# When x and the last halves of U's sums are loaded for the first pair of a Winograd-multiplied token MLP, and the buffer in which one end is made

## The chip, the cores and the metric

One core of one Trainium2 chip. The metric is the device time of one execution in microseconds (us); before the change the median of three runs is 703.48 us (702.54 to 704.59). Everything is float32; matrix products go through TensorE as fp32r, with each operand split into a high part and the rest, so that one product is three matmuls (high by high, high by rest, rest by high).

## The reference, cut to what matters

```
sa, ca, ga, sb, cb, gb = modulation rows made from c
h = layernorm(x) * (1 + ca) + sa            # x: 2048 tokens x 640 channels
x = x + ga * A(h, k, v, ...)                # short conv, gate, long conv by FFT
h = layernorm(x) * (1 + cb) + sb
u = gelu(h^T @ w1 + b1)                     # 640 x 1728, over the tokens
y = (u @ w2 + b2)^T                         # 2048 x 640
out = x + gb * y
```

The change lies in the last two lines: U times w2, and the ends `out = x + gb * (y + b2)`. By then x (after the first residual) is in DRAM, in `xs`.

## The kernel before, in words

Instructions stand in program order on each engine; nothing is rescheduled. Up to 503 us the kernel computes the convolution, the norms and U, one block of 128 of the 1728 hidden units after the other (`FS`, matmuls at L437). The last block ends at 515.8 us. From there on the matmuls at L1074 multiply U by w2, in eight **pairs** of 128-token blocks. A pair is a 2 x 2 block product, done with seven products instead of eight (Winograd's form). So a pair needs sums of w2's four quarters A11, A12, A21, A22 (`sums`, on VectorE), which are then split (`prep`: high part on ScalarE at L1011, rest on VectorE at L1012, shown as L60), and it needs sums of U's quarters (`TU`), made once.

**The products.** `product(n)` does the 56 products, seven for each pair: for n = 0 to 6 in the order A11, A12, S4, S1, S2, S3, A22 (`FIRST`). Each sums over seven sets of hidden units (`SETS`, three matmuls each, 21 in all) into one PSUM buffer. Products take the four PSUM buffers of a ring in turn: product n+4 writes where product n wrote, so it waits until product n has been read. The weights of product n+3 reuse the slot of those of product n.

**U's sums.** For the five sets 6, 0, 1, 2, 3 the sums were made early and saved to DRAM (`ts`), because there was no room. They come back (`t_back` L897, and L1051, L1064 for set 6) in ten transfers of 640 KB: first the halves `T13` (used by S1 and S3), then the halves `T42` (used by S2 and A22). The last two of the ten are set 3's second half, into `h_x` (L1063, shown as L897), and set 6's second half, into `m_x` (L1064). Product 4 (S2) is the first that reads the second halves. Sets 4 and 5 are made in place (`t_sums`, `t_split`), set 5 late, while the first products run.

**The ends.** `outcome(n)` follows product n. For the first pair: A11 is copied to `p1` by ScalarE (L1093); S1 to `p5` (L1095); A12 is finished by VectorE (`finish`: L1083, times gb, plus x at L1085) in the buffer `o1` and stored (L1086); S2's outcome makes `u2 = S2 + p1`, then `o1 = u2 + p5`, and finishes with it the bank of product 2 (S4), again in `o1`, plus x[1]; and so on. `p1, p5, u2, u3, o1` and the first of the x buffers are 320-column pieces of one tile, `m_w1`, so all of them appear in the trace as `m_w`.

**x.** `x_pair(p)` loads the four x pieces (160 KB each) of pair p; two sets of four buffers take turns. The second pair's last three buffers lie in `m_p`, over the working space of U's sums.

**SP's queue.** All transfers here are issued by SyncE (SP) in program order. In the built program every transfer has one of eight completion semaphores in turn, and SP issues a transfer only when the eighth before it has landed. SP also waits at a store until VectorE has made what is stored, with all later loads behind it. The order before, from the last sums on: ..., set 2's second half (`r_z`), `x_pair(0)` (4), set 3's second half, set 6's second half, A11 and A12 of pair 1 (4 transfers), `x_pair(1)` (4), the store of A12's end, A21 and A22 of pair 1 (4), the further stores.

Of the kernel before, what the change touches and what calls it, by code (L numbers as in the profile page):

```python
# [12 lines left out]
ALU = mybir.AluOpType  # L13
# [37 lines left out]
def mixer_kernel(ctx: ExitStack, tc: tile.TileContext, q, k, v, shift_k, ssm_k, ssm_D, w1, b1, w2, b2, c,  # L51
# [7 lines left out]
    act, dve, pool, pe, sync = nc.scalar, nc.vector, nc.gpsimd, nc.tensor, nc.sync  # L59
    TT = lambda eng, o, a, b, op: eng.tensor_tensor(o, a, b, op=op)  # L60
# [10 lines left out]
    def psum(slot=None):  # L71

        uid[0] += 1
        slot = ring[uid[0] % len(ring)] if slot is None else slot
        return psp.tile([128, 1024], F32, name=f"pst_{uid[0]}", tag=f"pst{slot}", bufs=1)
# [315 lines left out]
    def load_w2(t, s, f0):  # L391

        sync.dma_start(t[:, 0:6, :], dram(w2, fo(f0) * S + 128 * s, [[S, 128], [128 * S, 6], [1, 128]]))
        sync.dma_start(t[:, 6, :], dram(w2, fo(f0 + 6) * S + 128 * s, [[S, 128], [1, 128]]))
# [479 lines left out]
    def t_sums(i):  # L874

        hi, lo = full[7 + i]
        TT(dve, TW[:, 640:1280], hi, lo, ALU.add)
        TT(dve, T13, span2(TW, 320, 640), span2(TW, 0, 320), ALU.subtract)
        TT(dve, TW[:, 960:1280], TW[:, 960:1280], T13[:, 0], ALU.subtract)
        TT(dve, TW[:, 640:960], TW[:, 640:960], TW[:, 960:1280], ALU.subtract)  # L880
# [13 lines left out]
    def t_back(i, k):  # L894

        t, n = H[JS[i][k]][0], SAVED.index(i)
        sync.dma_start(bass.AP(tensor=t.tensor, offset=t.offset, ap=[t.ap[0], [1, 1280]]),  # L897
                       ts[128 * n:128 * n + 128, 1280 * k:1280 * k + 1280])

    def t_split(i):  # L900

        for k, t in enumerate((T13, T42)):
            act.activation(span2(H[JS[i][k]][0], 0, 640).bitcast(F32R), t, AF.Copy)
        for k, t in enumerate((T13, T42)):
            TT(dve, span2(H[JS[i][k]][0], 320, 640).bitcast(F32R), t, span2(H[JS[i][k]][0], 0, 640), ALU.subtract)
# [58 lines left out]
    def load_pair(p, n0=0, n1=4):  # L964

        if p < NP:
            for n in range(n0, n1):
                w_ = ("A11", "A12", "A21", "A22")[n]
                A[p, w_] = place[(4 * p + n) % 8]
                load_w2(A[p, w_], 2 * p + int(w_[1] == "2"), 7 * int(w_[2] == "2"))  # L970

    W, bank, slots, place = {}, {}, [], [q7(X, 0), q7(X, 896)]
    Q = lambda n, i: U[7 * (n // 2) + i]
    moving = {"A11": lambda i: Q(0, i)[0::2], "A12": lambda i: Q(2, i)[0::2], "S4": lambda i: Q(2, i)[1::2],
              "S1": lambda i: TU[i][0], "S2": lambda i: TU[i][1], "S3": lambda i: TU[i][2], "A22": lambda i: TU[i][3]}
    SETS = (4, 0, 1, 2, 3, 6, 5)
    FIRST = ("A11", "A12", "S4", "S1", "S2", "S3", "A22")
    ORDER = ("A11", "A12", "S1", "S2", "S3", "S4", "A22")
    of = lambda n: (n // 7, (ORDER if n > 6 else FIRST)[n % 7])
# [1 line left out]
    def x_load(s, h, t):  # L981
        sync.dma_start(t, xs[128 * s:128 * s + 128, 320 * h:320 * h + 320])

    def x_pair(p):
        if p < NP:
            for n in range(4):
                x_load(2 * p + n // 2, n % 2, xq[4 * (p % 2) + n])

    def sums(n):

        p, w_ = of(n)
        if p >= NP:
            return
        a = lambda k: A[p, k]
        if w_ == "S1":
            A[p, w_] = S1 if p else place[6]
            TT(dve, A[p, w_], a("A21"), a("A22"), ALU.add)
        elif w_ == "S2":
            TT(dve, a("A21"), a("A11"), a("A21"), ALU.subtract)
            TT(dve, a("A11"), a("S1"), a("A11"), ALU.subtract)  # L1000
            A[p, "S3"], A[p, "S2"] = a("A21"), a("A11")
        elif w_ == "S4":
            TT(dve, a("A12"), a("A12"), a("S2"), ALU.subtract)
            A[p, "S4"] = a("A12")

    def prep(n):

        p, w_ = of(n)
        if p < NP:
            W[n] = slots[n % 3]  # L1010
            act.activation(W[n][0].bitcast(F32R), A[p, w_], AF.Copy)  # L1011
            TT(dve, W[n][1].bitcast(F32R), A[p, w_], W[n][0], ALU.subtract)  # L1012

    for f_ in FS:
# [18 lines left out]
        if f_ == FS[-1]:  # L1033
# [13 lines left out]
            t_, n = thirds(m_x, 8, 1792), SAVED.index(6)  # L1047
# [11 lines left out]
    m_w1 = mem(f"w{WB[12]}", 4096, "m_w1")  # L1059
    p1, p5, u2, u3, o1, *xq = thirds(m_w1, 10, 896) + thirds(m_p, 3)  # L1060
    S1 = q7(m_w1, 0)
    x_pair(0)
    t_back(3, 1)  # L1063
    sync.dma_start(m_x[:, 3072:4352], ts[128 * n:128 * n + 128, 1280:2560])  # L1064
    load_pair(1, 0, 2)

    def product(n):
        w_ = of(n)[1]
        bank[n] = psum()[:, 0:320]
        wh, wl = W.pop(n)  # L1070
        for m, i in enumerate(SETS):
            rh, rl = moving[w_](i)
            for k, (w, r) in enumerate(((wh, rh), (wh, rl), (wl, rh))):
                pe.matmul(bank[n], w[:, i].bitcast(F32R), r.bitcast(F32R), start=m == 0 and k == 0,  # L1074
                          stop=m == 6 and k == 2)

    def finish(s, h, t, o, x, u=None):

        g = GB[:, 320 * h:320 * h + 320]
        if u is None:  # L1080
            dve.scalar_tensor_tensor(o, t, B2C[:, s:s + 1], g, op0=ALU.add, op1=ALU.mult)
        else:
            dve.scalar_tensor_tensor(o, t, B2C[:, s:s + 1], u, op0=ALU.add, op1=ALU.add)  # L1083
            TT(dve, o, o, g, ALU.mult)
        TT(dve, o, o, x, ALU.add)  # L1085
        sync.dma_start(out[128 * s:128 * s + 128, 320 * h:320 * h + 320], o)  # L1086

    def outcome(n):

        p, w_ = of(n)  # L1090
        t, s, x = bank[n], 2 * p, xq[4 * (p % 2):4 * (p % 2) + 4]
        if w_ == "A11":
            act.activation(p1, t, AF.Copy)  # L1093
        elif w_ == "S1":
            act.activation(p5, t, AF.Copy)  # L1095
        elif w_ == "A12":
            finish(s, 0, t, o1, x[0], p1)
        elif w_ == "S2":
            TT(dve, u2, t, p1, ALU.add)
            if p == 0:  # L1100
                TT(dve, o1, u2, p5, ALU.add)
                finish(s, 1, bank[2], o1, x[1], o1)
        elif w_ == "S3":
            TT(dve, u3, t, u2, ALU.add)
            if p:
                TT(dve, u2, u2, p5, ALU.add)
            finish(s + 1, 1, u3, p5, x[3], p5)
            if p == NP - 1:
                TT(dve, u3, u3, GB[:, 0:320], ALU.mult)
                TT(dve, u3, u3, x[2], ALU.add)  # L1110
        elif w_ == "S4":
            if p:
                finish(s, 1, t, u2, x[1], u2)
        elif p == NP - 1:
            finish(s + 1, 0, t, o1, u3)
        else:
            finish(s + 1, 0, t, u3, x[2], u3)

    for n in range(7 * NP):
        if n == 1:  # L1120
            t_sums(5)
        if n:
            prep(n + 2)
        if n == 1:
            t_split(5)
            x_pair(1)
        if n == 2:
            outcome(1)
        if n > 3:
            sums(n + 3)  # L1130
        product(n)
        if n != 1:
            outcome(n)
        if n == 2:
            load_pair(1, 2, 4)
        if n % 7 == 6:
            load_pair(n // 7 + 2)
            x_pair(n // 7 + 2)
# [6 lines left out]
def build(inputs):  # L1145
    import concourse.bacc as bacc

    nc = bacc.Bacc("TRN2", target_bir_lowering=False, num_devices=1)
    arrays, args = {}, []

    def add(name, a):
        a = np.ascontiguousarray(a)
        arrays[f"in_{name}_dram"] = a
        args.append(nc.dram_tensor(f"in_{name}_dram", a.shape, mybir.dt.from_np(a.dtype), kind="ExternalInput").ap())

    for name in _INS:
        a = np.asarray(inputs[name])
        add(name, a.reshape(S, D) if name in ('A_q', 'A_k', 'A_v') else a)
    for name, a in _constants().items():
        add("const_" + name, a)  # L1160
    args.append(nc.dram_tensor("out_0_dram", (S, D), F32, kind="ExternalOutput").ap())
    with tile.TileContext(nc) as tc:
        mixer_kernel(tc, *args)
    return nc, arrays
# [8 lines left out]
```

## Time and profile before

| | |
|---|---|
| median of three runs | 703.48 us (702.54 to 704.59) |
| the profiled execution's own time | 698.38 us |
| its span in the profile | 696.6 us |
| TensorE (PE) busy | 636.1 us, 91% |
| VectorE (DVE) busy | 510.4 us, 73% |
| ScalarE (ACT) busy | 312.7 us, 45% |
| mean granted TensorE clock | 0.98 (1.00 in every stretch from 440 us on) |

Lines of a timeline read: start (us), duration, engine, line, operation, out<-in, shapes, count; in brackets the engine's idle time before it and what released it. PE is the matmuls, PEld the weight loads beside them, SPq an issue on SP's queue; the duration of several issues in one line includes the waits between them. The chain of waits gives start, length and the work or the transfer that the end hung on. Matmul ends are modelled: starts are what to go by.

### The profile page before, as it was taken

Reading aid. Unit: us, or ns where it says so; the run is one execution under the profiler, and the core shown is the slowest. Engines: PE = TensorE matmul, PEld = TensorE weight load, DVE = VectorE, ACT = ScalarE, POOL = GpSimd, SP = SyncE. Lnnn points to the kernel's source line nnn. Section 1 sums busy time; section 2 is a strip of 40 time slices with the busy share of each in tenths; the row PEclk is TensorE's granted clock in tenths of the full one; section 3 lists DMA queues with packets and bytes.
Section 4 is the critical chain, followed back from the end, with each engine's and each line's share of the span. In section 5 each row is a group of like instructions: output and inputs, shape, how many; then the busy total and the mean of one; then the engine's idle time right before and its main releaser. Section 6 shows DMA issues by size and latency. Waiting matters only on the chain.

```text
span 696.6 us, 20710 instructions
## 1 busy us (share of the span) xinstructions
PE 636.1 (91%) x9057; PEld 615.6 (88%) x9057; DVE 510.4 (73%) x857; ACT 312.7 (45%) x467; POOL 154.9 (22%) x137
## 2 busy tenths in 40 slices
PE   0699978889999999987899999999998999999997
PEld 0699668889999989776899999999997999999997
DVE  7778559969879637888895420675586898988886
ACT  0664574635645545645766421532433333333331
POOL 5288039625526427200000000000000000000000
PEclk9999899999999899999999999999999999999999
DMA  9978888546333513352113651578499644455511
GB/s 183 218 221 256 303 159 169 129 78 145 69 65 87 174 45 82 116 135 49 30 32 59 124 97 25 128 182 216 148 320 302 182 127 128 130 171 173 162 49 39
DMA packets 173553, 95.91 MB, mean 138 GB/s; under 512 B 89716, under 2 KB 163223, under 8 KB 173463
## 3 DMA queue, kind: packets, MB, share of 16 engines
q1 hardware_dynamic: 168914, 93.28, 51.6%
q10 hardware_dynamic: 4548, 1.31, 1.1%
q8 instruction: 71, 1.16, 0.7%
q14 instruction: 20, 0.16, 0.1%
HBM read 77.53 MB, written 17.04 MB: 136 GB/s over the span
## 4 chain that ended last, share of the span: by engine, by line
PE 62%; DVE 15%; POOL 8%; DMA 7%; ACT 4%; issue 2%; SPq 2%; ACTq 0%; DVEq 0%; POOLq 0%
PE pst L1074 22%; PE pst L437 17%; PE pst L230 7%; POOL y L60 6%; PE pst L246 5%; PE pst L275 5%; PE pst L939 3%; DVE tap L60 3%; DMA aux<-in_A_ssm_k_dram 2%; DVE kt L60 2%; DMA h_a<-ts 1%; SPq L164 1%; DMA m_x<-ts 1%; POOL t L60 1%; DMA in<-in_A_k_dram 1%
## 5 line engine op out<-in xcount | busy, mean ns | idle before, releaser
L246 PEld LDWEIGHTS pst<-z,w 128*64 128x64 f32 x2560 | 94.7, 141 | 9.2 <-ACT z L232 7.3
L246 PE MATMUL pst<-z,w 128*64 128x64 f32 x2560 | 96.0, 240 | 7.5 <-ACT z L232 6.1
L60 POOL TENSOR_TENSOR y<-p 128x256 f32<-128x256 f32 x72 | 91.6, 1328 | 23.6 <-DVE p L60 23.2
L60 DVE TENSOR_TENSOR p<-pst,kt 128x512 f32<-128x512 f32 x80 | 52.5, 691 | 21.9 <-ACT kt L250 13.5
L230 PE MATMUL pst<-v,x 128*64 128x128 f32 x640 | 46.6, 307 | 23.5 <-DVE x L60 23.5
L230 PEld LDWEIGHTS pst<-v,x 128*64 128x64 f32 x640 | 44.6, 221 | 24.1 <-POOL t L462 23.5
L232 ACT ACTIVATE z<-pst 128x1024 f32<-128x1024 f32 x40 | 45.9, 1148 | 40.1 <-PE pst L230 22.2
L275 PEld LDWEIGHTS pst<-v,y 32*128 32x128 f32 x1280 | 40.4, 197 | 6.8 <-POOL y L60 3.6
L250 ACT ACTIVATE kt<-pst 128x512 f32<-128x512 f32 x40 | 25.2, 630 | 47.0 <-PE pst L246 24.9
L275 PE MATMUL pst<-v,y 32*128 32x64 f32 x1280 | 42.4, 283 | 3.6 <-DVE y L60 2.8
L1074 PE MATMUL pst<-r_z,m_w 128*128 128x320 f32 x198 | 37.5, 310 | 2.5 <-DVE m_w L1083 2.5
L230 PE MATMUL pst<-v,p 128*64 128x128 f32 x640 | 37.4, 274 | 2.3 <-ACT p L176 1.6
L230 PEld LDWEIGHTS pst<-v,p 128*64 128x64 f32 x640 | 35.1, 137 | 3.3 <-ACT p L176 1.7
L60 DVE TENSOR_TENSOR tap<-tap,kt 128x512 f32<-128x512 f32 x51 | 35.6, 698 | 1.3
L60 DVE TENSOR_TENSOR kt<-in,tap 128x512 f32<-128x512 f32 x51 | 35.0, 687 | 1.5
L1074 PEld LDWEIGHTS pst<-r_z,m_w 128*128 128x128 f32 x198 | 31.1, 188 | 2.9 <-issue 2.7
L283 ACT ACTIVATE z<-pst 128x512 f32<-128x512 f32 x38 | 21.3, 661 | 25.6 <-PE pst L275 25.6
L1011 ACT ACTIVATE m_w<-m_v 128x896 fp32r<-128x896 f32 x19 | 17.9, 949 | 25.9 <-DVE m_v L60 14.9
L1074 PE MATMUL pst<-h_x,m_w 128*128 128x320 f32 x132 | 26.5, 309 | 0.0
L294 PEld LDWEIGHTS pst<-z,v 64*64 64x64 f32 x1280 | 21.1, 139 | 5.8 <-issue 3.1
L437 PE MATMUL pst<-r_z,wb 128*128 128x320 f32 x144 | 23.1, 317 | 2.6 <-DVE aux L60 1.7
L60 DVE TENSOR_TENSOR m_w<-m_v,m_w 128x896 fp32r<-128x896 f32 x19 | 20.7, 1088 | 6.5 <-ACT m_w L1011 6.5
(300 smaller groups left out, 1426.0 us busy)
## 6 DMA issues: line engine op xcount, KB each, us to landing
x<-in_B_w_dram SPq DMA_DIRECT2D x20, 512.0 KB
m_v<-in_B_w_dram SPq DMA_DIRECT2D x20, 384.0 KB
aux<-in_A_ssm_k_dram SPq DMA_DIRECT2D x10, 512.0 KB
out_dram<-m_w SPq DMA_DIRECT2D x32, 160.0 KB
in<-in_A_k_dram SPq DMA_DIRECT2D x36, 128.0 KB
in<-in_A_v_dram SPq DMA_DIRECT2D x36, 128.0 KB
ts<-m_p SPq DMA_DIRECT2D x10, 320.0 KB
m_w<-xs SPq DMA_DIRECT2D x20, 160.0 KB
```

Source lines behind the costliest of these rows:

```text
L60: TT = lambda eng, o, a, b, op: eng.tensor_tensor(o, a, b, op=op)
L230: pe.matmul(ps[64 * ri:64 * ri + 64, o:o + 128], lhs, F1[:, 128 * ri:128 * ri + 128], start=True, stop=True)
L232: evac = lambda: act.activation(Z[:, side, t].rearrange("p a k e -> p e a k"), ps.rearrange("p (e a k) -> p e a k", a=8, e=2), AF.Copy)
L246: pe.matmul(ps[64 * h:64 * h + 64, o:o + 64], W2[k1 // 32][:, 2 * (k1 % 32) + ri], rhs, start=True, stop=True)
L250: act.activation(kt.rearrange("p (m i) -> p m i", i=32), pv[:, :, 1], AF.Copy)
L275: pe.matmul(pp[qd // 2][:, o:o + 64], Y[p, ri, i:i + 2].rearrange("p i k -> p (i k)"), V2[p, 64 * ri:64 * ri + 64], start=ri == 0, stop=ri ...
L283: act.activation(o, i, AF.Copy)
L294: pe.matmul(ps[64 * b:64 * b + 64, 512 * e + 64 * jj:512 * e + 64 * jj + 64], V1[p, ri, n2], T2[p, :, 32 * ri + n2], start=ri == 0, stop=r ...
L437: pe.matmul(ps[0:m, h, 0:320], w_.bitcast(F32R), r_[:, 320 * h:320 * h + 320].bitcast(F32R), start=first and i == 0, stop=last and i == 2)
L939: pe.matmul(ps[n][:, h, 0:320], sets[n][:, j].bitcast(F32R), r[:, 320 * h:320 * h + 320].bitcast(F32R), start=j == 0 and r is hh, stop=j = ...
L1011: act.activation(W[n][0].bitcast(F32R), A[p, w_], AF.Copy)
L1074: pe.matmul(bank[n], w[:, i].bitcast(F32R), r.bitcast(F32R), start=m == 0 and k == 0, stop=m == 6 and k == 2)
```

## The change

For the first pair, `x_pair(0)` is issued after the second halves of sets 3 and 6 instead of before them. `x_pair(1)` is issued after all four quarters of pair 1 (and so after the first store), instead of between A12 and the store. From product 4 on, set 6 (which lies in `m_x` for S1, S2, S3 and A22) is multiplied last and set 5 before it; products 0 to 3 keep the order. In the first pair S2's end is made in `p1` instead of `o1`.

```diff
-    SETS = (4, 0, 1, 2, 3, 6, 5)
+    SETS = (4, 0, 1, 2, 3)
...
     S1 = q7(m_w1, 0)
-    x_pair(0)
     t_back(3, 1)
     sync.dma_start(m_x[:, 3072:4352], ts[128 * n:128 * n + 128, 1280:2560])
+    x_pair(0)
     load_pair(1, 0, 2)
...
-        for m, i in enumerate(SETS):
+        for m, i in enumerate(SETS + ((6, 5) if n < 4 else (5, 6))):
...
             if p == 0:
-                TT(dve, o1, u2, p5, ALU.add)
-                finish(s, 1, bank[2], o1, x[1], o1)
+                TT(dve, p1, u2, p5, ALU.add)
+                finish(s, 1, bank[2], p1, x[1], p1)
...
         if n == 1:
             t_split(5)
-            x_pair(1)
...
         if n == 2:
             load_pair(1, 2, 4)
+            x_pair(1)
```

In the order of the built programs this moves the eight x loads on SP's queue and the last two sets of the products from the fifth on; the instructions on VectorE, ScalarE and GpSimd stand in the same order and number as before. The `p1` that the first pair's S2 end now occupies is written again by ScalarE's copy of A11 of the second pair (L1093), which therefore waits for that end's store.

## The prediction, on record before the changed kernel ran

> **What bounds the kernel now.** I read the windows first, for the stretch in which TensorE stops; then the chain of waits over the last 240 us, for what ends each stop; then the timelines of PE, VectorE and SP around it. Windows (us, then busy time and count of PE, PEld, DVE, ACT, POOL, then granted clock, DMA share, GB/s):
>
> ```profile
> 520.00:540.00 20.00, 16.63 (x112) 16.11 (x111) 13.98 (x21) 7.55 (x11) 0.00 (x0) 1.00 0.93 316
> ```
>
> PE stands for 3.37 us (20.00 - 16.63) while the first pair's products run, at full clock. The chain says why:
>
> ```profile
> 523.20 8.19 DMA m_x<-ts
> ...
> 532.80 3.62 DMA out_dram<-m_w
> ...
> 536.87 0.50 DVE m_w L60
> ...
> 537.40 0.56 DVE m_w L1083
> ...
> 538.10 154.49 PE pst L1074 x1050
> ```
>
> From 538.10 on the chain is PE's matmuls (154.49 us) and the last end behind them: what is won ahead of 538.10 is won at the end, as long as nothing else becomes late. PE's timeline, starts being what counts:
>
> ```profile
> 525.04 1.04 PE L1074 MATMUL pst<-r_z,m_w 128*128 128x320 f32 x6
> ...
> 528.12 0.60 PE L1074 MATMUL pst<-r_z,m_w 128*128 128x320 f32 x3
> ...
> 529.89 0.62 PE L1074 MATMUL pst<-h_x,m_w 128*128 128x320 f32 x3
> 531.43 0.70 PE L1074 MATMUL pst<-m_x,m_w 128*128 128x320 f32 x3 [0.92 <-DMA m_x<-ts]
> ...
> 538.10 0.68 PE L1074 MATMUL pst<-r_z,m_w 128*128 128x320 f32 x3 [2.45 <-DVE m_w L1083]
> ...
> 550.49 0.84 PE L1074 MATMUL pst<-r_z,m_w 128*128 128x320 f32 x3
> ```
>
> A product without a stop takes 528.12 - 525.04 = 3.08 us, a set of three matmuls 0.44. Product 4 starts at 528.12. Two stops follow: **stop A**, in product 4, until set 6's second half lands (531.43 where 529.89 + 0.44 = 530.33 was due: 1.10 us); **stop B**, ahead of product 6, until VectorE has read the bank of product 2 (L1083). Without stops product 6 would start at 528.12 + 2 x 3.08 = 534.28; it starts at 538.10, 3.82 later. A third, tiny one is in product 10 at 550.49: its first three matmuls take 0.84 for the usual 0.60, 0.24 us.
>
> **Part 1: S2's end in p1.** VectorE's timeline:
>
> ```profile
> 528.16 0.49 DVE L60 TENSOR_TENSOR m_w<-m_w 128x320 f32<-128x320 f32 x1
> 528.57 1.08 DVE L60 TENSOR_TENSOR m_x<-m_v,m_x 128x896 fp32r<-128x896 f32 x1
> 529.64 1.09 DVE L60 TENSOR_TENSOR m_w<-m_v,m_w 128x896 fp32r<-128x896 f32 x1
> ...
> 536.87 0.49 DVE L60 TENSOR_TENSOR m_w<-m_w 128x320 f32<-128x320 f32 x1 [3.77 <-DMA out_dram<-m_w]
> ...
> 538.92 1.08 DVE L60 TENSOR_TENSOR m_w<-m_v,m_w 128x896 fp32r<-128x896 f32 x1
> 539.92 0.48 DVE L60 TENSOR_TENSOR m_w<-pst,m_w 128x320 f32<-128x320 f32 x1
> 540.44 0.55 DVE L1083 SCALAR_TENSOR_TENSOR m_w<-m_w,sm 128x320 f32<-128x320 f32 x1
> ...
> 542.96 1.08 DVE L60 TENSOR_TENSOR m_w<-m_v,m_p 128x896 f32<-128x896 f32 x1
> ...
> 549.77 1.09 DVE L60 TENSOR_TENSOR m_w<-m_v,m_w 128x896 fp32r<-128x896 f32 x1 [1.08 <-ACT m_w L1011]
> ```
>
> 528.16 adds x[0] to A12's end in o1; its store is issued at 532.80 and out at 536.42 (3.62 in the chain); only then may 536.87 write o1 again, and L1083, which frees the bank, comes after it at 537.40. In p1 there is no store to wait for: p1's last reader is u2, one instruction earlier on the same engine. So stop B's cause goes. What is late next is VectorE's own queue.
>
> **Part 2: x behind the last halves.** SP's timeline:
>
> ```profile
> 516.62 3.75 SPq L982 DMA_DIRECT2D m_w<-xs  x4
> 521.64 0.32 SPq L897 DMA_DIRECT2D h_x<-ts  x1
> 523.20 0.32 SPq L1064 DMA_DIRECT2D m_x<-ts  x1
> 524.79 0.38 SPq L393 DMA_DIRECT2D m_v<-in_B_w_dram  x1
> 526.38 0.33 SPq L394 DMA_DIRECT2D m_v<-in_B_w_dram  x1
> 526.83 0.38 SPq L393 DMA_DIRECT2D m_v<-in_B_w_dram  x1
> ```
>
> Each issue waits for the eighth transfer before it, so issues tell landings: 521.64, 523.20, 524.79 and 526.38 are the landings of set 6's first half and of three further 640 KB halves, 1.58 us apart. The transfers move one behind the other at 655 KB / 1.58 us = 415 GB/s; the path is full, and issuing earlier gains nothing, only standing earlier in line does. 526.83 is the eighth after x[0], so x[0] landed at most 0.45 us after the half ahead of it. Now the line is: last r_z half 526.35, h_x 527.9, m_x 529.5 (before 531.4), x[0] 529.95, x[3] near 531.4, which is m_x's landing before (the same bytes in all).
>
> Stop A: m_x is now there at 529.5, and set 5 first puts its use at 529.89 + 0.88 = 530.77. It goes, with 1.3 us to spare. The reordered sets themselves cost nothing: the same 21 matmuls; h_x, needed at 529.89, lands at 527.9.
>
> The price: x[0]. Call T the start of its addition, 528.16 before, when x[0] had been there for 1.3 us. Now T is its landing: from 529.95 (above) to 531.4 (it cannot be later than x[3], whose place in the bytes is m_x's of before). I take T = 530.1, near the lower end, since 0.45 is the row nearest to it; 0.15 for the semaphore and for m_x's slowness at 531.38 where 1.58 steps give 531.1. So this is an added wait of some 1.9 us on VectorE. Queued behind it: the rest of prep(5) (528.57), that of prep(6), then S2's outcome. From the rows: prep(5)'s rest at T + 0.41 = 530.5, ending 531.6; prep(6)'s at T + 1.48; u2 at T + 2.48 (1.00 as from 538.92 to 539.92); the addition in p1 0.52 later (539.92 to 540.44), T + 3.00 = 533.1; L1083 at 533.6, ending 534.2. From the addition on everything stands 536.87 - 533.1 = 3.77 us earlier than before.
>
> PE: product 5 starts at 531.20; its third matmul (531.50) needs prep(5)'s rest at about 531.75: 0.25 lost. Product 6 could start at 534.53; the bank is free at 534.2 plus 0.14 (537.96 to 538.10): no wait. That is 3.57 gained, and 0.08 more from the first matmuls after stop B (0.68 for 0.60). Products 7 to 9 follow without a stop.
>
> Product 10 needs prep(10)'s rest: 549.77 before, the last of a VectorE queue that has no pause from 536.87 but the 1.08 us it waits for ScalarE behind its own sum. This queue moves by 3.77, PE by 3.65; before, PE lost 0.24 there, now 0.12. So the gain behind product 10 is that of the queue, **3.77 us**. It cannot exceed 3.82 + 0.24 = 4.06 (no stop at all), and with T = 531.4 it is 536.87 - 534.4 = 2.5.
>
> [...]
>
> **Part 3: x of the second pair behind its weights.** A21 and A22 are issued right behind the first store, x_pair(1) after them; as each waits for the eighth before, the last part of A22 waits for A11's first, which had landed by 533.07:
>
> ```profile
> 533.07 0.95 ACT L1011 ACTIVATE m_w<-m_v 128x896 fp32r<-128x896 f32 x1 [3.46 <-DMA m_v<-in_B_w_dram]
> ```
>
> So A22's last issue is near 533.1. VectorE first needs these quarters for S1's sum, 542.96 before, 539.2 now (less 3.77): 6 us behind the issue. x_pair(1), issued next, is first needed behind product 8, whose end PE reaches at 534.5 + 3 x 3.08 = 543.8. What hides both is that VectorE and PE have the first pair to work on; nothing gained, nothing lost. Were that cover gone, VectorE's queue would lose one for one.
>
> Part 3 also delays p1's store, behind x_pair(1) and T: made by 533.6 + 1.52 = 535.2 (537.40 to 538.92), landed near 538.8 by the 3.62 of the chain. ScalarE writes p1 again with product 7's outcome, which ends at 534.5 + 2 x 3.08 = 540.7. Covered by 1.9 us.
>
> **Sum.** 698.38 - 3.77 = 694.6 us for an execution like the profiled one (span 692.8); the median of the runs stood 5.1 above the profiled time, the same kernel: 703.48 - 3.7 = **699.8 us**. About 0.3%, 2.1 us, is what a measurement of this kernel can tell from no change.
>
> **Rivals.**
> *x[0] late* (0.10): the stop on PE is exchanged for one on VectorE. For it: each 160 KB load could pay a landing of its own instead of the 0.45; the isolated store took 3.62 from issue to landing, T = 529.5 + 3.62 = 533.1 and a gain of 0.8 us (702.7). Against: x[0] is issued between 516.62 and 521.64, at least 8 us ahead, while the line is full. Above T = 531.8 the gain is under 2.1. [...]
> *A21 and A22 late* (0.03), the side of slower: they stand behind a store that now waits for T. VectorE holds at S1's sum, 539.2, one for one; from a landing at 543.0 on the change is slower than before, by over 0.3% from 545.1 (705.6). Against: issued by 533.1, and the longest issue to landing in the chain's rows here is 8.19 (541.3, still a gain of 1.7).
> *m_x not earlier* (0.07): transfers share the engines and the move does nothing. Stop A shrinks only by the 0.44 of the swapped set, to 0.66; product 6 at 534.95, bank free by then: 3.15 + 0.08 + 0.24 = 3.5 us (700.0). Still faster: most of the gain is in part 1. With part 1 alone I get 535.5 for product 6, 2.6 + 0.3 = 2.9 us.
>
> **How the numbers follow.** The forecast has 0.80. Faster by over 0.3%: the forecast, the last rival and a little of the first, less what measuring blurs: 0.86. Same: most of the first: 0.11. Slower: 0.03. The range: gains of 4.06 down to 2.0 (the bound T = 531.4 and the near part of the first rival) give 699.4 to 701.5; the median of three runs itself is loose by some 0.6 us (702.54 to 704.59), so 698.8 to 702.0.
>
> **What would show it.** Right: no idle on PE ahead of m_x or product 6; the addition to u2 in VectorE's timeline without a transfer as releaser; at x[0]'s addition a wait for xs of about 2 us ending near 530; product 6 near 534.5. Wrong: x[0]'s addition after 531.8, an idle VectorE ahead of S1's sum or ScalarE ahead of L1093, or a gain lost again behind product 10.

## The result: both stops are gone; the whole executions moved by more than the change can explain

The first comparison: 694.37 us median of 4 runs (691.34 to 696.85), the kernel before 704.04 us (702.54 to 705.17), ratio 0.9862 with a 95% interval of 0.9815 to 0.9909: 9.7 us less where 3.7 was forecast, and below the forecast's range. Repeated in five rounds on one chip (e1): 698.43 us (10 runs, 694.26 to 700.65) against 700.79 us (32 runs, 697.25 to 705.73), ratio **0.9943, interval 0.9913 to 0.9974**. The two medians are 2.4 us apart; the ratio would be 4.0 us. The ratios are of fast runs only, without those more than 1.5% above the fastest of their kernel, and executions of this kernel lie further apart than that (three of the twelve of e2 are left out), which can tilt a ratio.

In the profile of after, the chain of waits from product 0 on is one piece:

```profile
514.99 172.49 PE pst L1074 x1176
```

The windows (columns as before): PE has no idle time where it had 3.37 us before.

```profile
520.00:540.00 20.00, 20.00 (x138) 20.00 (x138) 18.49 (x29) 7.75 (x10) 0.00 (x0) 1.00 0.92 305
```

PE's timeline, from product 4's first set: product 4 runs through (sets 3 and 5 in `h_x`, then set 6 in `m_x`), product 6 starts at 533.30, 2 x 3.08 behind product 4.

```profile
527.14 0.60 PE L1074 MATMUL pst<-r_z,m_w 128*128 128x320 f32 x3
...
528.90 1.04 PE L1074 MATMUL pst<-h_x,m_w 128*128 128x320 f32 x6
529.78 0.60 PE L1074 MATMUL pst<-m_x,m_w 128*128 128x320 f32 x3
...
533.30 0.60 PE L1074 MATMUL pst<-r_z,m_w 128*128 128x320 f32 x3
...
545.62 0.60 PE L1074 MATMUL pst<-r_z,m_w 128*128 128x320 f32 x3
```

VectorE's timeline: a new wait for x[0] (527.93), none for the store (530.95 is the addition in p1, right behind u2), and prep(10)'s rest at 543.86.

```profile
527.93 0.49 DVE L60 TENSOR_TENSOR m_w<-m_w 128x320 f32<-128x320 f32 x1 [1.06 <-DMA m_w<-xs]
528.34 1.08 DVE L60 TENSOR_TENSOR m_x<-m_v,m_x 128x896 fp32r<-128x896 f32 x1
529.34 1.08 DVE L60 TENSOR_TENSOR m_w<-m_v,m_w 128x896 fp32r<-128x896 f32 x1
530.42 0.49 DVE L60 TENSOR_TENSOR m_w<-pst,m_w 128x320 f32<-128x320 f32 x1
530.95 0.49 DVE L60 TENSOR_TENSOR m_w<-m_w 128x320 f32<-128x320 f32 x1
...
543.86 1.09 DVE L60 TENSOR_TENSOR m_w<-m_v,m_w 128x896 fp32r<-128x896 f32 x1 [1.08 <-ACT m_w L1011]
```

SP's timeline: each issue in the second half of these rows waits for the eighth transfer before it (1.2 us for the last `r_z` half, 0.8 for h_x's, 1.2 for m_x's), so the last `r_z` half landed by 524.23, h_x's by 525.81, m_x's by 527.39: 1.58 us apart, as before.

```profile
515.03 0.38 SPq L897 DMA_DIRECT2D h_x<-ts  x1
515.46 0.45 SPq L1063 DMA_DIRECT2D m_x<-ts  x1
516.36 5.03 SPq L982 DMA_DIRECT2D m_w<-xs  x4
522.64 0.38 SPq L393 DMA_DIRECT2D m_v<-in_B_w_dram  x1
524.23 0.74 SPq L394 DMA_DIRECT2D m_v<-in_B_w_dram  x1
525.81 0.38 SPq L393 DMA_DIRECT2D m_v<-in_B_w_dram  x1
527.39 0.70 SPq L394 DMA_DIRECT2D m_v<-in_B_w_dram  x1
```

All that the change touches lies behind product 0's first matmul. The measure used below is therefore the **stage**: from that matmul's start to the start of the last end (L1081), in one profile. 176.81 us before (515.80 to 692.61), 172.67 after (514.83 to 687.50): 4.14 us gained. (The expectations of e1 and e2 count to the end of that last end, 0.56 us further: 177.4 before.) 56 products of 3.08 us are 172.48, so of stops next to nothing is left. Another 0.97 us of the two profiles' difference lies ahead of product 0, where the two programs are the same. "First" is product 0's start.

| kernel | stage us | first us | median us (runs) |
|---|---|---|---|
| before; again in e2 | 176.81; 176.49 | 515.80; 520.28 | 700.79 (32); 700.81 (12) |
| after; again in e1 | 172.67; 174.08 | 514.83; 520.84 | 694.37 (4); 698.43 (10) |
| p1 only: e3; e11 | 173.83; 172.86 | 518.22; 518.46 | 698.21 (12); 697.04 (1) |
| moves and sets only: e4 | 175.20 | 511.59 | 700.79 (11) |
| after, old order of sets: e5 | 172.68 | 517.33 | 695.75 (1) |
| after, x_pair(0) as before: e6 | 172.68 | 519.78 | 698.19 (1) |
| after, x_pair(1) as before: e7 | 173.17 | 513.24 | 692.15 (1) |
| after, evacuation first: e8 | 172.68 | 520.82 | 698.95 (10) |
| after, late A21 and A22: e9 | 178.18 | 515.80 | 699.72 (1) |
| e9 with evacuation first: e10 | 175.11 | 528.25 | 709.10 (1) |
| p1 and evacuation first: e12 | 173.24 | 522.36 | 701.34 (1) |

### The profile page after: what moved, and what is told of

Same layout as the page of the kernel before. It is cut to its first block, busy times and chain, and to the rows that moved or that the text cites. A ratio compares the mean times of both kernels' runs of the same rounds, so it can differ in the third digit from the quotient of the medians.

```text
span 691.5 us, 20713 instructions
## 1 busy us (share of the span) xinstructions
PE 634.1 (92%) x9057; PEld 614.7 (89%) x9057; DVE 510.9 (74%) x857; ACT 312.4 (45%) x467; POOL 155.3 (22%) x137
## 4 chain that ended last, share of the span: by engine, by line
PE 67%; DVE 14%; POOL 8%; ACT 4%; issue 3%; SPq 2%; DMA 1%; ACTq 0%; DVEq 0%; POOLq 0%
PE pst L1074 25%; PE pst L437 18%; PE pst L230 7%; POOL y L60 6%; PE pst L246 5%; PE pst L275 5%; PE pst L939 3%; DVE tap L60 3%; PE pst L294 2%; DVE kt L60 2%; POOL t L60 1%; SPq L164 1%; DMA in<-in_A_k_dram 1%; PE tap L354 1%; DVE y L60 1%
## 5 line engine op out<-in xcount | busy, mean ns | idle before, releaser
L230 PE MATMUL pst<-v,x 128*64 128x128 f32 x640 | 45.1, 300 | 23.8 <-DVE x L60 23.6
L230 PEld LDWEIGHTS pst<-v,x 128*64 128x64 f32 x640 | 43.3, 222 | 24.3 <-POOL t L462 23.6
L275 PEld LDWEIGHTS pst<-v,y 32*128 32x128 f32 x1280 | 39.6, 193 | 7.1 <-POOL y L60 4.3
L275 PE MATMUL pst<-v,y 32*128 32x64 f32 x1280 | 41.6, 279 | 4.1 <-DVE y L60 3.2
L230 PE MATMUL pst<-v,p 128*64 128x128 f32 x640 | 37.3, 274 | 2.9 <-issue 1.7
L230 PEld LDWEIGHTS pst<-v,p 128*64 128x64 f32 x640 | 35.0, 137 | 3.9 <-issue 2.2
L294 PE MATMUL pst<-z,v 64*64 64x64 f32 x1280 | 24.2, 231 | 2.8 <-issue 1.7
```

Source lines behind the costliest of these rows:

```text
L230: pe.matmul(ps[64 * ri:64 * ri + 64, o:o + 128], lhs, F1[:, 128 * ri:128 * ri + 128], start=True, stop=True)
L275: pe.matmul(pp[qd // 2][:, o:o + 64], Y[p, ri, i:i + 2].rearrange("p i k -> p (i k)"), V2[p, 64 * ri:64 * ri + 64], start=ri == 0, stop=ri ...
L294: pe.matmul(ps[64 * b:64 * b + 64, 512 * e + 64 * jj:512 * e + 64 * jj + 64], V1[p, ri, n2], T2[p, :, 32 * ri + n2], start=ri == 0, stop=r ...
```

## The experiments

**e1, the changed kernel again**, and **e2, the kernel before again** (a comment line added).

> The changed kernel once more, unaltered. Theory M (the change removes the two stops of the first pair and nothing else): from the start of product 0 to the end the profile shows 172.5 to 173 us where the kernel before has 177.4, a gain of 4.1 us, and the median time is 4 to 4.5 us below that of the kernel before, ratio 0.993 to 0.995; the 9.7 us of the first comparison were executions that differ in the 500 us ahead of the change. Theory N (the timed executions stop longer at these two places than the profiled one did): the ratio is again near 0.986, 9 to 10 us.

> The kernel before once more, unaltered, as a control. Theory M: its executions spread over several us although nothing differs, and its profile shows the differences ahead of product 0 (512 to 520 us for its start), not behind it (177.4 us within 0.3). Theory N: the part behind product 0 varies by several us between executions, up to 183 us where the profile before had 177.4. Median within 1 us of the kernel before under both.

Theory N is out: e1 is 2.4 us (medians) to 4.0 us (ratio) below the kernel before and not 9 to 10. That the times alone show the 4.1 us of theory M can't be said. The control e2 shows what executions do on their own: 12 runs of an unaltered kernel from 693.19 to 707.79, the median equal (700.81 to 700.79), and yet a ratio to itself of 0.995 (0.9912 to 0.9988), an interval that misses 1. By this measure e1 (0.9943), p1 only (0.9947, 0.9914 to 0.9981), the moves only (0.9935, 0.9896 to 0.9973, with a median equal to that of the kernel before) and the unaltered kernel can't be told apart. What tells them apart is the stage: e2's is 176.49 where the other profile had 176.81, while its first matmul of product 0 came 4.48 us later. So in the profiled executions the spread lies ahead of product 0. It goes with the granted clock. Windows of the same stretch of the convolution, e2 and then e7, with PE counted as busy throughout in both:

```profile
235.00:240.00 5.00, 5.00 (x123) 4.88 (x121) 4.96 (x6) 2.74 (x4) 0.00 (x0) 0.72 0.37 95
240.00:245.00 5.00, 5.00 (x76) 4.67 (x72) 0.81 (x4) 2.08 (x3) 0.00 (x0) 0.50 0.58 121
```

```profile
235.00:240.00 5.00, 5.00 (x131) 4.81 (x128) 4.64 (x5) 3.56 (x6) 0.00 (x0) 1.00 0.58 131
240.00:245.00 5.00, 5.00 (x139) 4.93 (x136) 0.00 (x0) 2.31 (x5) 0.00 (x0) 1.00 0.39 82
```

The same 128 matmuls (L275) took 7.11 us in e2, from 242.33 on, and 3.93 us in the first profile of after, from 240.72 on, where the clock was 1.00 in both windows, as in e7. Summed over the windows of 5 us between 20 and 310 us, the granted clock falls short of 1.00 by 3.45 us in e7 and by 25.6 us in e10, and product 0 starts at 513.24 and at 528.25; over the fourteen profiles the two figures have a correlation of 0.94.

Over all runs with a recorded mean clock (104 in eight groups) the time falls by 4.7 us for each 0.01 of clock; within a group the correlation is -0.65 to -0.94. The first four runs of after had a mean clock of 0.9835, the ten of e1 0.9776; 0.0059 of clock are 2.8 us of the 4.1 us between these two sets. Brought to the same clock, 0.977, by this slope, the kernel before stands at 701.2 to 702.0 (three groups), after at 697.3 (the first four runs) and 698.7 (e1), p1 alone at 698.3, the moves alone at 699.8, with standard errors of 0.4 to 0.8: a gain of some 2.5 to 4.7 us for the change.

e1's stage was 1.4 us longer than expected, and its profile says where. VectorE waited 2.64 us for A21 and A22 of the first pair ahead of product 0 (0.45 in the first profile of after); S4's sum and split came late, the evacuation of U's last block (reading it out of PSUM, `u_evac`) stood behind the split on ScalarE, and product 1's last set, set 5, waited for it. VectorE, then PE:

```profile
520.14 1.09 DVE L60 TENSOR_TENSOR m_v<-m_v 128x896 f32<-128x896 f32 x1 [2.64 <-DMA m_v<-in_B_w_dram]
```

```profile
527.03 0.41 PE L1074 MATMUL pst<-h_x,m_w 128*128 128x320 f32 x1 [0.31 <-ACT h_x L848]
527.89 0.56 PE L1074 MATMUL pst<-h_x,m_w 128*128 128x320 f32 x2 [0.45 <-DVE h_x L60]
```

**e3, p1 only**, and **e11, the same again.**

```diff
-                TT(dve, o1, u2, p5, ALU.add)
-                finish(s, 1, bank[2], o1, x[1], o1)
+                TT(dve, p1, u2, p5, ALU.add)
+                finish(s, 1, bank[2], p1, x[1], p1)
```

> The kernel before with S2's end made in p1 and nothing else. Theory M: the stop ahead of set 6 (about 1.1 us) stays, the stop ahead of product 6 goes; 2.9 us less than before from product 0 to the end. Theory N: most of 9 us.

> The kernel before with S2's end in p1 and nothing else, once more: in e3 the late loads of A21 and A22 hid what p1 alone leaves. Expected: no stop ahead of product 6; ahead of set 6 in product 4 between nothing and 1.1 us, as the line of transfers falls; VectorE ahead of S1's sum up to 1.2 us, as in e7, since x_pair(1) stands ahead of A21 and A22. 172.7 to 174.3 us from product 0 to the last end (176.5 to 176.8 before), or 1.3 us more if VectorE again idles over 2 us for m_v.

e3 met the same late loads as e1 (2.40 us of idle VectorE, a stop in product 1); PE was then late enough that set 6's second half was there: no stop in product 4, against the expectation. e11 had them in time (0.69 us): stage 172.86, 3.6 to 3.95 us less than the two profiles of before. No stop ahead of product 6, which starts 6.34 us behind product 4, and next to none at set 6; the addition in p1 has no releaser. p1 alone carries nearly all of the gain. e11's PE (products 4 and 6) and VectorE, then e2's PE with the stop that p1 takes away:

```profile
530.78 0.60 PE L1074 MATMUL pst<-r_z,m_w 128*128 128x320 f32 x3
...
537.12 0.60 PE L1074 MATMUL pst<-r_z,m_w 128*128 128x320 f32 x3
```

```profile
534.76 0.49 DVE L60 TENSOR_TENSOR m_w<-m_w 128x320 f32<-128x320 f32 x1
```

```profile
534.91 0.71 PE L1074 MATMUL pst<-m_x,m_w 128*128 128x320 f32 x3
...
542.25 0.68 PE L1074 MATMUL pst<-r_z,m_w 128*128 128x320 f32 x3 [3.12 <-DVE m_w L1083]
```

**e4, everything but p1.**

```diff
-                TT(dve, p1, u2, p5, ALU.add)
-                finish(s, 1, bank[2], p1, x[1], p1)
+                TT(dve, o1, u2, p5, ALU.add)
+                finish(s, 1, bank[2], o1, x[1], o1)
```

> The changed kernel with S2's end in o1 again: the loads of x moved and the sets swapped, nothing else. Theory M: no stop ahead of set 6; VectorE waits for the first store to leave o1. That store is now issued at once behind its end (528.5 in the changed kernel's profile, 532.80 before) and is out 3 to 5 us later, so product 6 waits 0 to 2 us instead of 2.45 and the gain from product 0 to the end is 2 to 4 us. If the p1 buffer is what counts, only the 1.1 us of the first stop are gained. Theory N: 6 us or more.

175.20: 1.3 to 1.6 us gained, less than expected. The store is issued 13.65 us behind product 0's start (525.24), 17.00 before (532.80), since x_pair(1) no longer stands ahead of it, and still VectorE waits 3.13 us for it and PE 1.81.

```profile
531.06 0.49 DVE L60 TENSOR_TENSOR m_w<-m_w 128x320 f32<-128x320 f32 x1 [3.13 <-DMA out_dram<-m_w]
```

```profile
532.28 0.68 PE L1074 MATMUL pst<-r_z,m_w 128*128 128x320 f32 x3 [1.81 <-DVE m_w L1083]
```

From issue to the end of the wait the 160 KB store took 531.06 - 525.24 = 5.8 us, in a line of loads.

**e5, the old order of sets; e6, x_pair(0) at its old place; e7, x_pair(1) at its old place**, each in the changed kernel.

```diff
# e5
-        for m, i in enumerate(SETS + ((6, 5) if n < 4 else (5, 6))):
+        for m, i in enumerate(SETS + (6, 5)):
# e6
+    x_pair(0)
     t_back(3, 1)
...
-    x_pair(0)
# e7
             t_split(5)
+            x_pair(1)
...
             load_pair(1, 2, 4)
-            x_pair(1)
```

> The changed kernel with the old order of the last two sets (6, then 5) in all products. In the changed kernel's profile set 6's second half lands 0.25 us behind the start of product 4, and the old order would use it at 2.2 us. Expected: no stop in product 4, 172.5 to 173 us from product 0's first matmul to the last end, as in the changed kernel (172.67). If the order of the sets carries part of the gain: a stop of 0.4 us or more ahead of m_x. The profile also gives one more pair of numbers for the time ahead of product 0: with granted clock lost between 20 and 310 us near 8.5 us product 0 starts near 512 to 515, near 12 to 15 us at 520 or later.

> The changed kernel with the first pair's x loaded ahead of the last two halves, as before. These halves then land 1.6 us later: set 6's second half 1.8 to 3.3 us behind the start of product 4, due at 2.64. Expected: a stop of 0 to 0.7 us in product 4, and no wait of VectorE for x[0]; 172.6 to 173.5 us from product 0 to the last end. If where x stands in line is what counts: over 174.

> The changed kernel with the second pair's x loaded behind A12 again, ahead of the first store and of A21 and A22. Expected: no change, 172.5 to 173 us, since with p1 no end waits for that store; A21 and A22 are issued some 2 us later, near 533 in the changed kernel's times, and are needed at 537. If this move carries part of the gain: VectorE idle ahead of S1's sum (m_w<-m_v,m_p), and up to 2 us more.

e5 and e6: 172.68 each, no stop. Neither the sets nor the place of the first x earned anything in these executions. In e6 set 6's second half, 1.6 us later in line, was still there at 534.74, where the new order first reads it in product 4 (no bracket; issued at 526.07):

```profile
534.74 0.60 PE L1074 MATMUL pst<-m_x,m_w 128*128 128x320 f32 x3
```

They can save at most stop A, 1.1 us, where the line of transfers falls late, as in the profile of before; in e2, the same kernel, stop A was down to 0.1 us and stop B up to 3.12. No run here met the late line with only one of these parts. e7 lost 0.5 us: behind x_pair(1), A22 of the second pair came late to S1's sum, VectorE's queue moved, and product 10 waited. The move of x_pair(1), which the prediction priced at nothing, is worth this in that execution; e12 below lost about the same, e11 0.2 with a wait of 0.42 us at S1's sum.

```profile
536.75 1.09 DVE L60 TENSOR_TENSOR m_w<-m_v,m_p 128x896 f32<-128x896 f32 x1 [1.20 <-DMA m_p<-in_B_w_dram]
```

```profile
544.71 0.41 PE L1074 MATMUL pst<-r_z,m_w 128*128 128x320 f32 x1 [0.22 <-DVE m_w L60]
```

**e8, the evacuation of U's last block ahead of prep(2)**; **e9, late A21 and A22; e10, both; e12, p1 with the evacuation first.**

```diff
# e8 (e10 and e12 too)
             sums(2)
+            u_evac(f_, ps)
             prep(2)
-        u_evac(f_, ps)
+        else:
+            u_evac(f_, ps)
# e9 (e10 too)
             t_back(0, 0)
-            load_pair(0, 2, 4)
...
                 t_back(i, 0)
+                if i == 1:
+                    load_pair(0, 2, 4)
```

> The changed kernel with the last block of U evacuated ahead of the splitting of S4's weights instead of behind it (ScalarE's queue and VectorE's). In e1 and e3, A21 and A22 of the first pair landed 2 us later against product 0 than in the other runs; S4's sum and split were late, the evacuation stood behind them, and product 1's last set waited 1.2 to 1.4 us. Expected: 172.5 to 172.8 us from product 0 to the last end whether these loads are early or late; the median near that of the changed kernel, 0.994 of the kernel before, within what executions differ by (some 2 us for a median). If the evacuation's place is not the cause: in a run with VectorE idle over 2 us for m_v, product 1 still stops.

> The changed kernel with A21 and A22 of the first pair issued one 640 KB half later (behind t_back(1, 0)), so that they land some 1.6 us or more later in every execution. Expected, if the stop of e1 and e3 comes from these loads: VectorE idle 2 to 4.5 us for m_v, product 1 stops 1 to 3.5 us ahead of its last set (h_x), 174 to 176.5 us from product 0 to the last end. If not: no stop, 172.7.

> The same late loads, with the evacuation of U's last block ahead of the split of S4's weights. Expected: no stop in product 1; product 2 waits for S4's weights only as far as they are later than 6.2 us behind product 0's start, 0 to 2 us; 172.6 to 174.5 us. If the evacuation's place is not what made the stop: as e9.

> S2's end in p1 and the last block of U evacuated first, no load moved. Expected: 172.7 to 174.3 us whether the loads of A21 and A22 are early or late; no stop in product 1. If the moved loads of the change are worth more than 1 us in every execution: over 174.

e8's profile had the loads in time (0.58 us), so it shows only that the new place costs nothing: 172.68; its median, 698.95 against 701.35 (13 runs), ratio 0.9957 (0.991 to 1.0004), tells it from after as little as from before. e9 issues the loads one 640 KB half later, and makes e1's stop: VectorE idle 5.32 us, product 1's last set at 524.67 where 521.52 (520.64 + 0.88) was due. The stage lost 5.5 us, more than expected: 3.9 in the stop (3.15, and 0.72 for the rest of h_x), 1.6 because the clock was then halved for some 3.4 us (0.83 in 526 to 527, 0.50 from 527 to 530, 0.97 in 530 to 531): nine matmuls took 2.37 us for the usual 1.48, six 1.74 for 1.04. VectorE, PE, and windows of e9:

```profile
517.77 1.09 DVE L60 TENSOR_TENSOR m_v<-m_v 128x896 f32<-128x896 f32 x1 [5.32 <-DMA m_v<-in_B_w_dram]
```

```profile
520.64 1.04 PE L1075 MATMUL pst<-u_y,m_w 128*128 128x320 f32 x6
524.67 0.41 PE L1075 MATMUL pst<-h_x,m_w 128*128 128x320 f32 x1 [2.98 <-ACT h_x L848]
525.53 0.56 PE L1075 MATMUL pst<-h_x,m_w 128*128 128x320 f32 x2 [0.45 <-DVE h_x L60]
...
526.37 2.37 PE L1075 MATMUL pst<-u_i,m_x 128*128 128x320 f32 x9
528.53 1.74 PE L1075 MATMUL pst<-u_y,m_x 128*128 128x320 f32 x6
```

```profile
526.00:527.00 1.00, 1.00 (x8) 1.00 (x7) 0.96 (x2) 0.00 (x0) 0.00 (x0) 0.83 1.01 410
527.00:528.00 1.00, 1.00 (x5) 1.00 (x4) 0.93 (x3) 0.74 (x1) 0.00 (x0) 0.50 0.96 383
```

With the evacuation first (e10) the same late loads (VectorE idle 4.92 us) cost 2.4 us instead of 5.5: the stop is split over product 1, 2 and 3 (0.81, 0.52, 0.31 us of idle PE) and no half clock follows (behind the second, nine matmuls take 1.49 us). More than expected, since VectorE's part of the evacuation still stands behind S4's sums. e12, which moves no load: 173.24, with the lost half us of e7 (VectorE 1.08 us at S1's sum), not over 174: in these two executions the moved loads were worth about 0.5 us.

## Why the prediction was right in its mechanism and wrong in its number

**The step that failed is the last one, from the profile to the median.** The prediction set the median of three runs, 703.48, as the level, called it loose by some 0.6 us, and took 2.1 us for what a measurement can tell from no change. The kernel before, run 63 times in all, spans 693.2 to 709.0 with a standard deviation of 3.2 us and a median of 701.0; two medians of four drawn from these 63 differ by up to 3.3 us either way in 8 of 10 draws. Against that, a range of 3.2 us was far too narrow, whatever the gain. That the profiled execution of before stood 5.1 us below the median was seen and taken as a fixed distance; it was this spread.

Of the 9.7 us of the first comparison, 3.0 lie on the side of before (704.04 against 701.0 over all its runs), 4.1 on the side of after (694.37 against 698.43 in e1), and 2.6 are left between those two. Why both sides fell apart in this way is explained only in part: the clock accounts for some 2.8 of the 4.1 us, and for the four runs of before no clock is on record. Such a difference came up in 1 of 100 draws of the 63 runs with 4.1 us taken off one side, so these runs were not typical of what came later. Of the four runs of after only one has a trace, and this stays open.

Point by point, against product 4's start (528.12 before, 527.14 after):

- *Stop B goes with p1*: right. Product 6 starts 6.16 us behind product 4 (predicted 6.41, before 9.98).
- *Stop A goes with the moves*: right in the profile of after, but not shown to be the moves' doing: e2, e11 and e12, with these loads and sets in the old order, have 0.1 us of it or less, and e3 none (its PE was itself late). It was counted as a fixed 1.1 us and is a matter of when the line falls. Nor do the two stops simply add: product 6 waits for the store, so in e2, without stop A, stop B was longer (3.12 for 2.45) and product 6 started 9.65 us behind product 4, where 9.98 stood with stop A. The one profile that the prediction was read from had a late line: its last r_z half landed 10.58 us behind product 0's start, against 9.40 to 10.19 in the profiles of after, e1, e2, e3, e4 and e6, whose first-pair weights were issued where they were before.
- *T, x[0]'s landing*: predicted 1.98 us behind product 4's start, measured 0.79. The line's steps were right: 1.58 us for each half, x[0] 0.54 behind m_x's (0.45 to 0.60 in the sum). What was off is the line's start: the last r_z half, which the change does not touch, landed 9.40 us behind product 0's start instead of 10.58. So VectorE lost 1.06 us there and not 1.9, and prep(5) cost PE nothing. The wait itself is not the price: in e8 VectorE reached this addition earlier, waited 2.08 us, and lost nothing by it (172.68), as x[0] was there 0.69 us behind product 4's start.

```profile
533.83 0.49 DVE L60 TENSOR_TENSOR m_w<-m_w 128x320 f32<-128x320 f32 x1 [2.08 <-DMA m_w<-xs]
```

- *The 2.0 us at which the range's gains end*: no run shows it. By the sum's own steps it takes x[0] at 536.87 - 2.0 - 3.00 = 531.87, 2.4 us behind the 529.5 for m_x. In the profile of after 0.54 us lay between the two, for 160 KB that would move in 0.39 at the 415 GB/s of the halves (an estimate from their 1.58 us), and the stage gained 4.14 us.
- *Product 10 and VectorE's queue*: the third stop went too, product 10 starts 18.48 us behind product 4, exactly six products. So x[0], charged with 0.29 us through VectorE's queue, cost nothing, and the gain was the whole 4.06 of the bound and the 0.08 of the first matmuls, 4.14, and not 3.77. (The bound had left out these 0.08, which the prediction counts one step earlier.)
- *x_pair(1), "nothing gained, nothing lost"*: wrong by up to 0.5 us (e7, e12). Before, VectorE reached S1's sum at 542.96, late enough; with stop B gone it comes earlier, and A22 behind x_pair(1) would be the next to be late. The move is the cover for the gain of p1.
- *Part 1 alone 2.9 us*: too low, 3.6 to 3.95 (e11), since stop A, which it left standing, was hardly there.
- The rivals with late x[0], late A21 and A22 of pair 1 (the second pair) and an unmoved m_x did not come about in the profile of after.

## What to carry to other kernels

When a value is written to a buffer that a store has just been given, look for a buffer whose last reader is the engine's own previous instruction: this removed a stop that moving every load around it could not (1.3 to 1.6 us against 3.6 to 3.95). Before forecasting a median, ask how far executions of the same kernel lie apart; where that is as much as the gain, compare a stage in the profiles, from the first instruction that the change can touch. And after a stop is gone, ask which load will next be the late one: here it was A22 of the second pair (VectorE idle 1.20 us in e7).

## What the runs showed of the hardware

A stop of PE of 2.45 us (before) or 3.12 us (e2) was followed by matmuls at full clock (1.00 in 538 to 540 of before; six matmuls in 1.04 us behind either stop); in e9, 3.15 us of stop and 0.72 more soon after were followed by some 3.4 us at 0.50 (rows above). PE's two idle stretches in e9, 2.98 and 0.45 us, are each shorter than e2's 3.12 and together 3.43; what brought the lower clock, these rows don't settle. Not expected was the convolution: PE counted as busy for all of 5.00 us in 235 to 240, and the granted clock 0.72 in one execution (e2) and 1.00 in another (the first of after), in the same run of matmuls (L275, L230), with PE idle for only 0.71 and 0.70 us ahead of it. By the correlation above these stretches go with most of what the profiled executions differ by. No run here shows what starts them.
